# A Fourier layer and two expert layers on one core: raw weights on GpSimd's queue, the tenth chunk of x inside the loop, decode steps and low parts of the first expert block on other engines

## The chip, the core and the metric

One core of a Trainium2 chip runs the whole program. Its engines each work through a list of instructions in order: TensorE (PE; PEld is its weight load), VectorE (DVE), ScalarE (ACT), GpSimd (POOL) and SyncE (SP), which here only issues transfers. ScalarE and GpSimd issue transfers too. The metric is the time of one execution in microseconds of the device, the median of several runs.

## The reference

```python
def _attn_ref(x, w_r, w_i, b_r, b_i):
    X = np.fft.rfft(x, axis=1)
    Yr = Xr @ w_r - Xi @ w_i + b_r
    Yi = Xr @ w_i + Xi @ w_r + b_i
    # soft threshold of both by 0.01
    return np.fft.irfft(Y, n=x.shape[1], axis=1)

def _moe_ref(x, w_in, w_out):
    h = x @ w_in
    return (h - np.tanh(h)) @ w_out

def _moe2_ref(x, w_in, w_out):
    h = x @ w_in
    return (h * np.clip(h + 3.0, 0.0, 6.0) / 6.0) @ w_out
```

The three are applied one after the other. x is 2 x 3008 x 256 in float32, the expert weights are 256 x 2048 and 2048 x 256 in float64.

## The kernel before

**The Fourier layer** runs in four stages: A (47 points, `dft_a`, one chunk of x at a time, 16 chunks, the result stored to DRAM as s1), B (64 points, `dft_b`, on rows read back from s1 into the tiles bi), the linear layer with its threshold (`linear`, `shrink`), C (`dft_c`, stored as s2) and D (`dft_d`). The first eight chunks (batch 0) come before the loop; chunks 8 to 15 (batch 1) share three tiles x1 (called xb in the rows), so chunk i+3 can be loaded only when chunk i is stored. A loop of 24 rounds (t) then runs `linear(t)`, `dft_c(t-2)`, `dft_b(t+2)` and, in the first rounds, one more `dft_a` (from chunk `A0` on, with both halves copied by ScalarE and stored on ScalarE's queue). A chunk before `A0` is stored by a line of its own. Constants of stages B and C come in pieces; those of C on GpSimd's queue, each behind a one-element copy (`gate`) that waits for a tile of the round.

**Every product in the expert layers** is three passes of float32r: high x high, high x low, low x high (lines 112 to 114), so each operand is split: ScalarE writes the high part (line 108, or 446), VectorE or GpSimd subtracts it from the source for the low part (line 109, or 451).

**The expert layers** run in 16 blocks of tokens (k) and 8 groups of hidden units (g), as 2 x 2 block products with seven multiplications (p1 to p7) in place of eight. A group makes al, be and ga in PSUM; ScalarE copies s1, s5 and su out of them (lines 633, 637, 645), VectorE adds them up to c11, c12 and c22 (635, 647, 655), and each of these goes through the nonlinearity (`nl`: ScalarE's activation, line 468, then VectorE's subtraction, line 469) and a split (`nl_split`). The four output products of group g run on TensorE within group g+1. The fourth sum, c21, stays in al and is treated at the start of the next group (`tail_nl`). A bank's next product can start only when ScalarE's copy of the last one is done. GpSimd prepares operands of the next block (`prep_early`: subtractions of line 428, low parts of line 451).

**The weights** arrive as raw 64-bit numbers (512 KB pieces, three buffers) and are decoded to float32 and split by a generator, `w_steps`, one step a call: ScalarE rescales the high words (line 165) and converts the low ones (168), VectorE masks (170), merges (183), adds (199), forms the sums for the block products (203 to 207); ScalarE writes the high part (180), VectorE the low part (191). Where `fine` holds, the steps are smaller. Steps are called at places of the loop's rounds until `NDEC` pieces are done, and then at the places a to e of a group (`super_hook`). A raw piece is asked for when the merge of an earlier one is on its way (`due`, `w_flush`).

## Time and profile before

| | |
|---|---|
| median of 3 runs | 1187.01 us (1186.61 to 1188.89) |
| the profiled execution | 1187.16 us |
| its span, first to last instruction | 1185.4 us |
| TensorE busy | 1174.0 us |
| VectorE, ScalarE, GpSimd busy | 927.4, 864.8, 170.5 us |
| TensorE's granted clock, all stages | 1.00 of full speed (2.4 GHz) |
| spectral loop and what leads to it | up to 163.9 us |
| first expert block, groups 1 to 7 | 163.9 to 220.5 us |

Busy time of TensorE overlaps from one matmul to the next, so a full share doesn't tell how much it waits. The stretches in which a matmul starts later than the step from one to the next are read from the timeline: start, duration, engine, line, what is written and read, and in square brackets how long the engine was idle before it and what ended that.

### The profile page before, as it was taken

Reading aid. Unit: us, or ns where it says so; the run is one execution under the profiler, and the core shown is the slowest. Engines: PE = TensorE matmul, PEld = TensorE weight load, DVE = VectorE, ACT = ScalarE, POOL = GpSimd, SP = SyncE. Lnnn points to the kernel's source line nnn. Section 1 sums busy time; section 2 is a strip of 40 time slices with the busy share of each in tenths; the row PEclk is TensorE's granted clock in tenths of the full one; section 3 lists DMA queues with packets and bytes.
Section 4 is the critical chain, followed back from the end, with each engine's and each line's share of the span. In section 5 each row is a group of like instructions: output and inputs, shape, how many; then the busy total and the mean of one; then the engine's idle time right before and its main releaser. Section 6 shows DMA issues by size and latency. Waiting matters only on the chain.

```text
span 1185.4 us, 20708 instructions
## 1 busy us (share of the span) xinstructions
PE 1174.0 (99%) x7750; PEld 1158.3 (98%) x7750; DVE 927.4 (78%) x1785; ACT 864.8 (73%) x1808; POOL 170.5 (14%) x176
## 2 busy tenths in 40 slices
PE   8999999999999999999999999999999999999998
PEld 6999999999999999999999999999999999999998
DVE  2589888888888888888877788777777777777776
ACT  2566777787778777777777778777777777777775
POOL 0000010202030111102021412121203030302100
PEclk9999999999999999999999999999999999999999
DMA  8986532012122213122106521000000000010000
GB/s 298 330 310 210 166 93 63 27 63 70 69 76 76 94 58 112 62 72 71 54 1 222 175 95 37 15 28 28 28 28 28 28 26 29 2 54 2 19 9 28
DMA packets 43948, 96.51 MB, mean 81 GB/s; under 512 B 4327, under 2 KB 27879, under 8 KB 43751
## 3 DMA queue, kind: packets, MB, share of 16 engines
q1 hardware_dynamic: 39113, 76.58, 19.5%
q0 software_dynamic: 2864, 13.24, 3.4%
q10 hardware_dynamic: 1870, 5.36, 1.3%
q8 instruction: 61, 1.00, 0.3%
q14 instruction: 40, 0.33, 0.1%
HBM read 58.72 MB, written 36.44 MB: 80 GB/s over the span
## 4 chain that ended last, share of the span: by engine, by line
PE 92%; DVE 3%; DMA 2%; ACT 2%; issue 1%; SPq 0%; ACTq 0%; DVEq 0%
PE acc L112 16%; PE acc L114 16%; PE acc L113 16%; PE al L112 7%; PE al L113 7%; PE al L114 7%; PE be L112 4%; PE be L113 4%; PE be L114 4%; PE ga L112 2%; PE ga L114 2%; PE ga L113 2%; PE ga L414 2%; PE acc L371 1%; DMA s<-xa 1%
## 5 line engine op out<-in xcount | busy, mean ns | idle before, releaser
L109 DVE TENSOR_TENSOR gl<-g,gh 128x376 fp32r<-128x376 f32 (+2 forms) x509 | 291.9, 573 | 154.7 <-ACT gh L108 131.6
L108 ACT ACTIVATE gh<-g 128x376 fp32r<-128x376 f32 (+2 forms) x509 | 262.8, 516 | 153.1 <-DVE g L469 81.1
L113 PE MATMUL acc<-wo,gh 128*128 128x256 f32 x752 | 211.9, 282 | 0.0
L112 PE MATMUL acc<-wo,gh 128*128 128x256 f32 x752 | 211.6, 281 | 0.0
L114 PE MATMUL acc<-wo,gl 128*128 128x256 f32 x752 | 211.3, 281 | 0.0
L112 PE MATMUL acc<-gh,wo 128*128 128x376 f32 x512 | 173.6, 339 | 0.0
L114 PE MATMUL acc<-gh,wo 128*128 128x376 f32 x512 | 171.2, 334 | 0.0
L113 PE MATMUL acc<-gl,wo 128*128 128x376 f32 x512 | 171.0, 334 | 0.0
L114 PEld LDWEIGHTS acc<-wo,gl 128*128 128x128 f32 x752 | 142.8, 190 | 0.0
L113 PEld LDWEIGHTS acc<-wo,gh 128*128 128x128 f32 x752 | 141.9, 189 | 0.0
L112 PEld LDWEIGHTS acc<-wo,gh 128*128 128x128 f32 x752 | 141.7, 188 | 0.0
L471 ACT ACTIVATE e<-c,three 128x384 f32<-128x384 f32 (+1 forms) x192 | 116.6, 607 | 12.7 <-DVE c L647 12.5
L472 DVE SCALAR_TENSOR_TENSOR g<-e,c 128x384 f32<-128x384 f32 (+1 forms) x192 | 105.6, 550 | 15.5 <-ACT e L471 10.5
L469 DVE TENSOR_TENSOR g<-c,e 128x376 f32<-128x376 f32 x189 | 113.8, 602 | 5.0 <-ACT e L468 2.4
L428 POOL TENSOR_TENSOR bmt<-bmt 128x376 f32<-128x376 f32 (+2 forms) x60 | 72.0, 1205 | 289.3 <-ACT bmt L419 289.1
L468 ACT ACTIVATE e<-c 128x376 f32<-128x376 f32 x189 | 97.4, 516 | 11.6 <-DVE c L647 11.2
L112 PEld LDWEIGHTS acc<-gh,wo 128*128 128x128 f32 x512 | 96.3, 188 | 0.0
L113 PEld LDWEIGHTS acc<-gl,wo 128*128 128x128 f32 x512 | 96.3, 188 | 0.0
L114 PEld LDWEIGHTS acc<-gh,wo 128*128 128x128 f32 x512 | 96.2, 188 | 0.0
L637 ACT ACTIVATE s<-be 128x376 f32<-128x376 f32 (+2 forms) x127 | 61.7, 486 | 43.3 <-PE be L114 42.9
L647 DVE TENSOR_TENSOR c<-be,su 128x376 f32<-128x376 f32 (+2 forms) x127 | 69.5, 548 | 19.7 <-ACT su L645 14.9
L645 ACT ACTIVATE su<-al 128x376 f32<-128x376 f32 (+2 forms) x127 | 60.6, 477 | 12.2 <-PE al L114 12.1
(219 smaller groups left out, 2792.0 us busy)
## 6 DMA issues: line engine op xcount, KB each, us to landing
raw<-in_moe_w_in_dram SPq DMA_DIRECT2D x16, 512.0 KB
raw<-in_moe_w_out_dram SPq DMA_DIRECT2D x16, 512.0 KB
w2id<-wout SPq DMA_DIRECT2D x8, 896.0 KB
wi<-w2id POOLq DMA_DIRECT2D x8, 896.0 KB, 4.8
y1d<-y SPq DMA_DIRECT2D x32, 188.0 KB
s<-co SPq DMA_DIRECT2D x23, 256.0 KB
bi<-s SPq DMA_DIRECT2D x11, 512.0 KB
bmt<-y1d SPq DMA_DIRECT2D x7, 768.0 KB
```

Of the source, the lines that this page charges most:

```text
L108: act.activation(out=hi, in_=src, func=ACTF.Copy)
L109: (lo_eng or dve).tensor_tensor(out=lo, in0=src, in1=hi.bitcast(F32), op=ALU.subtract)
L112: pe.matmul(out=out_ap, lhsT=lh, rhs=rh, start=start, stop=False, **kw)
L113: pe.matmul(out=out_ap, lhsT=lh, rhs=rl, start=False, stop=False, **kw)
L114: pe.matmul(out=out_ap, lhsT=ll, rhs=rh, start=False, stop=stop, **kw)
L428: eng.tensor_tensor(out=blkv(k, out), in0=blkv(k, a), in1=blkv(k, b), op=ALU.subtract)
L468: act.activation(out=e, in_=src, func=ACTF.Tanh)
L469: dve.tensor_tensor(out=g, in0=src, in1=e, op=ALU.subtract)
L471: act.activation(out=e, in_=src, func=ACTF.Relu, bias=three)
L472: dve.scalar_tensor_tensor(out=g, in0=e, scalar=6.0, in1=src, op0=ALU.min, op1=ALU.mult)
L637: act.activation(out=s5, in_=be, func=ACTF.Copy)
L647: dve.tensor_tensor(out=c12, in0=be, in1=su, op=ALU.add)
```

## The change

Four things are changed. (1) `A0` is 9: the tenth chunk's transform (chunk 9) moves from before the loop into round 0, its load from ScalarE's queue to SP's, behind the loads of the stored rows bi0 and bi1; the load of chunk 12 moves behind round 0. (2) Until the expert layers begin, raw weights are asked for on GpSimd's queue instead of SP's. (3) In block 0 the decode steps are counted as owed, one at each of a, b and d of a group and two at c, and a step that begins with ScalarE runs only at b or c, one at each; the generator says by what it yields whether its next step is one. `fine` holds from the 14th piece on instead of the 18th, so the rescaling and the conversion of a piece are steps apart. (4) In block 0 the low parts of g11 and g12 are made by GpSimd instead of VectorE.

```diff
@@ -128,13 +128,13 @@
 
-    A0 = 10
+    A0 = 9
     NDEC = 13
...
     w_raw = {}
-    ptr = {"load": 0, "dec": 0, "due": 0}
+    ptr = {"load": 0, "dec": 0, "due": 0, "owed": 0, "scalar": None}
 
@@ -143,7 +143,7 @@
             raw = wst.tile([128, 512], I64, tag="raw", bufs=3, name="raw")
-            sp.dma_start(out=raw, in_=w_src[nm][c].rearrange("p a f -> p (a f)"))
+            (sp if mo else pool).dma_start(out=raw, in_=w_src[nm][c].rearrange("p a f -> p (a f)"))
             w_raw[nm, c] = raw
@@ -154,7 +154,7 @@
         for k, (nm, c) in enumerate(w_order + [(None, 0)]):
-            fine = k > 16
+            fine = k > 12
             if nm:
@@ -164,12 +164,12 @@
                 if fine:
-                    yield
+                    yield True
                 act.activation(out=rnd, in_=lw, func=ACTF.Copy, scale=2.0 ** -29)
-                yield
+                yield not fine
                 dve.tensor_scalar(out=hw, in0=hw, scalar1=0x80000000, scalar2=None, op0=ALU.bitwise_and)
                 if fine:
-                    yield
+                    yield True
             if prev:
@@ -197,7 +197,7 @@
             dve.tensor_tensor(out=ta, in0=ta, in1=rnd, op=ALU.add)
-            yield
+            yield nm[1] == "o"
             src = taf
@@ -206,14 +206,14 @@
                 src = ws[:, 1:8, :].rearrange("p a f -> p (a f)")
-                yield
+                yield True
             n = src.shape[1]
...
     def w_step():
-        next(w_gen, None)
+        ptr["scalar"] = next(w_gen, None)
 
@@ -645,7 +645,7 @@
         dve.tensor_tensor(out=c12, in0=be, in1=su, op=ALU.add)
-        nl_split(k, g, 0, 0, g11)
+        nl_split(k, g, 0, 0, g11, None if k else pool)
         hook("b")
@@ -655,7 +655,7 @@
             g12 = nl(k, c12)
-        nl_split(k, g, 0, 1, g12)
+        nl_split(k, g, 0, 1, g12, None if k else pool)
         g22 = nl(k, c22)
@@ -705,13 +705,13 @@
                 f(a)
-        load_x(9, q=act)
         load_bm(1, act)
...
         load_bi(1)
+        load_x(9)
         dft_a(8)
@@ -725,7 +725,6 @@
         wpool["r"] = ctx.enter_context(tc.tile_pool(name="wr", bufs=1, side="right", reuse_waits="tile"))
-        ab = dft_a(9, False)
         dft_b(0)
@@ -734,11 +733,8 @@
         evict_b_neg(1)
-        dft_a_out(9, ab)
-        store_a(9)
         load_x(11)
         w_load()
-        load_x(12)
         ab = None
@@ -748,8 +744,7 @@
                 dft_b(t + 2)
-            if t:
-                ab = dft_a(a_next, False) if a_next < 16 else None
+            ab = dft_a(a_next, False) if a_next < 16 else None
             if t > 1:
@@ -780,8 +775,7 @@
                 load_cm(t // 2 + 1, s_t[t][0:1, 0, 0:1])
-            if t > 0:
-                load_x(12 + t)
+            load_x(12 + t)
             if t < 2:
@@ -879,9 +873,16 @@
                     prep_early(n, g, pos)
-            if 1 <= g < 6 and k < NS:
-                if k or pos in "abcd" and ptr["dec"] < 16:
-                    w_step()
+            if k == 0 and pos != "e":
+                ptr["owed"] += 2 if pos == "c" else 1
+                free = pos in "bc"
+                for _ in range(min(2, ptr["owed"])):
+                    if ptr["dec"] < 16 and (free or not ptr["scalar"]):
+                        free = free and not ptr["scalar"]
+                        w_step()
+                        ptr["owed"] -= 1
+            if 1 <= g < 6 and 0 < k < NS:
+                w_step()
             if pos == "e" and k in (NS - 1, NS):
```

TensorE ahead of the loop, before (xb1 is chunk 9, xb0 chunk 8, warm a filler):

```order
L688 MATMUL acc_209<-warm_120 128x256 x5
L275 MATMUL al_220<-xb0_100,amt_99 96x256 x2
L275 MATMUL be_223<-xb0_100,amt_99 96x256 x2
L688 MATMUL ga_240<-warm_120 128x256 x2
L275 MATMUL acc_247<-xb1_101,amt_99 96x256 x2
L275 MATMUL acc_250<-xb1_101,amt_99 96x256 x2
L319 MATMUL al_253<-bmt_82,bi0_87 128x128 x4
L319 MATMUL ga_264<-bmt_82,bi0_87 128x128 x4
```

and now:

```order
L688 MATMUL acc_208<-warm_120 128x256 x5
L275 MATMUL al_220<-xb0_100,amt_99 96x256 x2
L275 MATMUL be_223<-xb0_100,amt_99 96x256 x2
L688 MATMUL ga_240<-warm_120 128x256 x2
L319 MATMUL al_247<-bmt_82,bi0_87 128x128 x4
L319 MATMUL ga_258<-bmt_82,bi0_87 128x128 x4
```

The two B stages on bi0 follow the filler directly; chunk 9's four matmuls stand behind the third B stage, in round 0.

ScalarE in the fourth group of block 0 (c11, c12, c22 the sums, gh a high part, ws a decode buffer), before:

```order
L468 ACTIVATE e_1995<-c11_1989 128x376
L165 ACTIVATE ws_1999<-raw_1471 128x512
L168 ACTIVATE ws_1999<-raw_1471 128x512
L645 ACTIVATE su_2014<-al_1971 128x376
L108 ACTIVATE gh_2018<-g_1996 128x376
L180 ACTIVATE wi7_2023<-ws_1826 128x896
L468 ACTIVATE e_2036<-c12_2016 128x376
L108 ACTIVATE gh_2018<-g_2037 128x376
```

and now:

```order
L468 ACTIVATE e_1995<-c11_1989 128x376
L645 ACTIVATE su_2011<-al_1971 128x376
L108 ACTIVATE gh_2015<-g_1996 128x376
L165 ACTIVATE ws_2019<-raw_1471 128x512
L468 ACTIVATE e_2032<-c12_2013 128x376
L108 ACTIVATE gh_2015<-g_2033 128x376
L468 ACTIVATE e_2038<-c22_2030 128x376
L168 ACTIVATE ws_2019<-raw_1471 128x512
```

The rescaling stands behind the first split instead of ahead of su, the conversion behind the second, and the high part of a weight goes to the next group.

GpSimd over block 0 and the preparation of block 1 (bmt are operands, odd block 1's split ones), before:

```order
L109 TENSOR_TENSOR gl_1759<-bi1_88,gh_1758 128x376
L428 TENSOR_TENSOR bmt_82<-bmt_82 128x376 x2
L451 TENSOR_TENSOR odd_2286<-bmt_82,odd_2286 128x376 x3
L428 TENSOR_TENSOR bmt_82<-bmt_82 128x376
L451 TENSOR_TENSOR odd_2286<-bmt_82,odd_2286 128x376
```

and now, from the fifth group on:

```order
L109 TENSOR_TENSOR gl_2203<-g_2183,gh_2202 128x376
L109 TENSOR_TENSOR gl_2203<-g_2220,gh_2202 128x376
L428 TENSOR_TENSOR bmt_82<-bmt_82 128x376 x2
L451 TENSOR_TENSOR odd_2280<-bmt_82,odd_2280 128x376
L109 TENSOR_TENSOR gl_2300<-g_2277,gh_2299 128x376
L109 TENSOR_TENSOR gl_2300<-g_2320,gh_2299 128x376
L451 TENSOR_TENSOR odd_2280<-bmt_82,odd_2280 128x376 x2
L428 TENSOR_TENSOR bmt_82<-bmt_82 128x376
L109 TENSOR_TENSOR gl_2402<-g_2379,gh_2401 128x376
L451 TENSOR_TENSOR odd_2280<-bmt_82,odd_2280 128x376
L428 TENSOR_TENSOR bmt_82<-bmt_82 128x376
L109 TENSOR_TENSOR gl_2402<-g_2420,gh_2401 128x376
```

Two low parts a group now stand in GpSimd's list, and the two subtractions behind those of the fifth group.

## Rows read from the trace of the kernel before

**Rows 1.** The head of the page.

```profile
span 1185.4 us, 20708 instructions
```

**Rows 2.** Timeline of the start: start us, duration us, engine, line, what.

```profile
24.20 1.40 SPq L308 DMA_DIRECT2D bi<-s  x3
...
27.10 1.94 PE L275 MATMUL acc<-xb,amt 128*96 128x256 f32 x8 [1.65 <-DMA xb<-in_x_dram]
...
29.23 0.18 POOL L676 COPY gate<-bi 1x1 f32<-1x1 f32 x1 [28.78 <-DMA bi<-s]
...
29.27 1.13 PE L319 MATMUL al<-bmt,bi 128*128 128x128 f32 x8 [0.22 <-issue]
```

**Rows 3.** Timeline of TensorE in the loop: stage C of four rounds.

```profile
50.51 0.81 PE L371 MATMUL acc<-ly,cmt 128*128 128x256 f32 x3
...
56.85 0.81 PE L371 MATMUL acc<-ly,cmt 128*128 128x256 f32 x3
...
100.18 1.03 PE L371 MATMUL acc<-ly,cmt 128*128 128x256 f32 x4
...
104.81 1.03 PE L371 MATMUL acc<-ly,cmt 128*128 128x256 f32 x4
```

**Rows 4.** Timeline: chunks 11 and 12 asked for, a store, chunk 11 used.

```profile
32.67 0.32 SPq L259 DMA_DIRECT2D xb<-in_x_dram  x1
...
34.92 0.33 ACTq L296 DMA_DIRECT2D s<-xb  x1
...
44.93 0.31 SPq L259 DMA_DIRECT2D xb<-in_x_dram  x1
...
45.92 1.03 PE L275 MATMUL be<-xb,amt 128*96 128x256 f32 x4
```

**Rows 5.** Stretches: us, busy by engine (count), TensorE's clock, DMA share, GB/s.

```profile
24.00:26.00 2.00, 1.45 (x7) 0.92 (x5) 1.37 (x3) 1.39 (x3) 0.00 (x0) 1.00 0.78 283
...
40.00:45.00 5.00, 5.00 (x35) 4.63 (x34) 1.96 (x4) 2.02 (x5) 0.00 (x0) 1.00 0.93 314
```

**Rows 6.** DMA issues: destination and source, queue, count, size of one.

```profile
raw<-in_moe_w_in_dram SPq DMA_DIRECT2D x16, 512.0 KB
...
xb<-in_x_dram ACTq DMA_DIRECT2D x1, 512.0 KB
```

**Rows 7.** Timeline of ScalarE and of TensorE near 72 us.

```profile
70.05 0.67 ACT L165 ACTIVATE ws<-raw 128x512 f32<-128x512 f32 x1 [1.58 <-DMA raw<-in_moe_w_out_dram]
...
72.67 1.10 PE L275 MATMUL al<-xb,amt 128*96 128x256 f32 x4 [0.34 <-ACT xb L288]
```

**Rows 8.** Timeline of TensorE, first expert block: its start, a wait, its end.

```profile
163.91 0.34 PE L112 MATMUL al<-even,wi 128*128 128x376 f32 x1
164.08 0.33 PE L113 MATMUL al<-even,wi 128*128 128x376 f32 x1
...
186.03 0.44 PE L112 MATMUL al<-t3h,wi 128*128 128x376 f32 x1 [0.67 <-ACT su L645]
...
220.46 0.33 PE L112 MATMUL al<-odd,wi 128*128 128x376 f32 x1
```

**Rows 9.** Timeline of ScalarE in the first expert block.

```profile
180.06 0.52 ACT L108 ACTIVATE gh<-g 128x376 fp32r<-128x376 f32 x1 [1.46 <-DVE g L469]
...
181.72 0.52 ACT L108 ACTIVATE gh<-g 128x376 fp32r<-128x376 f32 x1 [0.73 <-DVE g L469]
...
184.39 0.66 ACT L165 ACTIVATE ws<-raw 128x512 f32<-128x512 f32 x1
...
185.50 0.47 ACT L645 ACTIVATE su<-al 128x376 f32<-128x376 f32 x1
```

**Rows 10.** Timeline: low parts on GpSimd and on VectorE.

```profile
164.93 0.99 POOL L109 TENSOR_TENSOR gl<-bi,gh 128x376 fp32r<-128x376 f32 x1 [76.45 <-ACT gh L108]
...
167.38 1.31 DVE L109 TENSOR_TENSOR gl<-g,gh 128x376 fp32r<-128x376 f32 x1
...
180.62 0.55 DVE L109 TENSOR_TENSOR gl<-g,gh 128x376 fp32r<-128x376 f32 x1 [0.58 <-ACT gh L108]
```

## The prediction

> **What bounds the kernel now.** I began with the busy shares and the chain that ended last, and both give TensorE nearly the whole span, which is 1185.4 us [rows 1]. A busy TensorE is not yet one at its best, so I then read its own timeline, for starts that stand further apart than the usual step: 0.17 us from one 376-column matmul to the next (163.91, 164.08) [rows 8]. Few do. At the start TensorE waits 1.65 us for the tenth chunk of x, which lands at 27.10, and 0.22 us more until the first stored rows (bi) are there [rows 2]. In the spectral loop it waits once, at 72.67, some 0.5 us beyond the step. In the first expert block it waits several times: the seven groups from 163.91 to 220.46 take 56.55 us [rows 8]; a group has 45 such matmuls, 7 x 45 x 0.172 = 54.2, so 2.3 us are waiting. Behind that, nothing that the change touches waits. All that it can win is therefore 2.3 + 0.5 us, and what it makes of the start; the rest of the question is what it costs.
>
> **The start.** Before, the tenth chunk's transform stands on TensorE ahead of the first B stage, which begins at 29.27; the stored rows that it needs were asked for at 24.20, and GpSimd's gate copy, which waits for the same rows, runs at 29.23 [rows 2]. So rows and transform are ready together. The change takes the transform away from there, and its 512 KB [rows 6] away from in front of the rows. The B stage then waits for the rows alone. At the rate of that moment, 283 GB/s [rows 5], 0.524 MB are 1.85 us, so the rows land between 29.23 - 1.85 = 27.4 (all of it was in their way) and 29.2 (none). I take 27.7, near the early end, since the chunk was asked for ahead of the rows and landed ahead of them. The transform isn't gone: it becomes part of the loop's first round. A round with a transform takes 56.85 - 50.51 = 6.34 us, one without 104.81 - 100.18 = 4.63 [rows 3], so it costs 1.71 there, and the loop has no slack to hide it. Sum: 27.7 + 1.71 - 29.27 = **+0.14 us** (-0.16 to +1.65). What was a free filling of a wait is now paid, and the wait's end comes earlier by about as much.
>
> **The twelfth chunk.** The raw weights leave SP's queue for GpSimd's. On SP the first of them stood behind the twelfth chunk of x (asked for at 32.67) and behind a thirteenth that waits until 44.93 for a store that ScalarE asked for at 34.92, ten microseconds for one store: the transfers are that crowded [rows 4]. On GpSimd's queue three of them, 512 KB each [rows 6], hang on gates alone: the first is asked for with the first stored rows, the other two some 8 us after it, by my estimate 5 to 10 us sooner than on SP's. They take turns with SP's transfers while those still carry two large stores and the twelfth chunk. TensorE used that chunk at 45.92 without a wait [rows 4]. No row shows when it landed. By the bytes asked for since 24.20, at the rates of the windows, the engines on the average reach its end at about 43, and the slowest later, perhaps just ahead of 45.92. One raw chunk ahead of it costs 0.524 MB at 314 GB/s [rows 5] = 1.7 us, two cost 3.3. With the start's +0.14 TensorE wants it at 46.06. So the wait is between 0 (it had 3 us of slack) and 3.2 (none, two chunks ahead). I take **+0.8 us**: nearly one chunk ahead of it, about half of that in slack. It would not be won back, since the loop is bound by TensorE from there on.
>
> **The wait at 72.67.** TensorE waits for ScalarE's copy of the transform; ScalarE had itself waited 1.58 us, until 70.05, for a raw chunk [rows 7], which SP had asked for late since it was stuck behind a chunk of x. GpSimd's queue has only gates and constants in it, and no load of x. I count **-0.5 us** (0 to -0.5).
>
> **First expert block, what goes.** ScalarE's two rescaling steps stood between the activation of c11 and the copy su: 184.39 to 185.50 [rows 9], and TensorE, which reuses that bank, started at 186.03 instead of 185.2, 0.8 us late [rows 8]. They are now taken apart and put behind the two splits of the group, one at each, where su is already done. VectorE loses two low parts a group, 0.55 us each [rows 10]. And GpSimd's two subtractions for the next block, which before ran far ahead, at the block's start, and stretched VectorE's low part at 167.38 to 1.31 us [rows 10], now stand behind the low parts, at the fifth group. All of this together could end all 2.3 us.
>
> **First expert block, what comes.** A low part takes 0.99 us on GpSimd [rows 10]. That VectorE's ran 1.31 us instead of 0.55 while GpSimd worked shows that they exclude each other: 0.76 us lost in one meeting. So the subtraction that follows on VectorE (it reads c and e, both in SBUF) must wait for GpSimd's low part. ScalarE's second split of a group and the next one are 181.72 - 180.06 = 1.66 us apart now [rows 9]; with a low part of 0.99 in between and VectorE's step released only then, I make it 2.04, +0.38 a group. The chain through a group (activations, subtractions, splits, back to the copy s) was about 6.8 us, and is 7.2 then, under the 45 x 0.172 = 7.75 that TensorE takes. It holds in a group without decode work on VectorE. Where a decode burst of some 2 us follows (third and fifth group) it doesn't: I find waits of 0.4 and 0.24 us there when I lay the rows' durations one behind the other. In groups six and seven GpSimd's queue now has the two subtractions, four low parts of the next block's operands, two more subtractions and the four low parts moved to it: twelve pieces of about a microsecond in two groups, 15.5 us. They meet VectorE at nearly every step; the same laying out gives TensorE waits of 0.5 and 0.75 us in the seventh group, which has none now. With 0.18 that stays at the start, 0.18 + 0.4 + 0.24 + 1.25 = 2.1 us of waiting against 2.3: **-0.2 us**. Bounds: -1.9 (only the 0.4 is left) to +1.7 (the last groups cost twice that, and the next block starts on a late operand).
>
> The Trainium skill says of this in "SBUF — State Buffer", "Who interferes with whom", that a VectorE instruction with two SBUF inputs and a GpSimd instruction that reads SBUF shut each other out for a whole instruction, whichever comes second. The trace agrees: 1.31 us against 0.55. By that rule alone, with every moved low part blocking VectorE and none fitting beside its PSUM reads, the block would be the rival below.
>
> Nothing else moves the time: the banks of the transforms change places with one another, the decode steps of later blocks stand where they stood, and a gate copy of GpSimd in front of a raw load waits for a step of the same round.
>
> **Sum.** The profiled execution took 1187.16 us, 0.15 over the median of 1187.01. 1187.16 + 0.14 + 0.8 - 0.5 - 0.2 = 1187.40; against the median, 1187.01 + 0.24 = 1187.25, which I round to **1187.3 us**.
>
> **Rivals.**
> The crowded start (slower): raw weights on GpSimd's queue take turns with SP's transfers, the twelfth chunk lands after 48.5 and TensorE waits 2.5 to 3.2 us. For it: no engine is idle of transfers there (314 GB/s at 40 to 45 us, [rows 5]). Against it: the slack isn't known. It decides from a wait of about 2.5 us; with 3.2, 1187.01 + 0.14 + 3.2 - 0.5 - 0.2 = 1189.7. Chance 0.13. The Trainium skill states in "DMA: Bandwidth & Descriptors", "Issuing engines are not separate DMA queues", that transfers of all queues run on the same 16 engines and interleave; by that rule another queue brings no bandwidth, and this rival is its price. The ten microseconds of ScalarE's store beside SP's full queue agree [rows 4].
> The lock in the last groups (slower): the twelve pieces on GpSimd cost TensorE 3 us there and at the next block's start rather than 1.25, so the block is at +1.7 to +2: 1187.01 + 0.14 + 0.8 - 0.5 + 2 = 1189.5. For it: 0.76 us in a single meeting [rows 10]. Against it: VectorE steps that read PSUM lie beside most pieces. Chance 0.13.
> The block cleared and the chunk in time (faster): 1187.01 + 0.14 - 0.5 - 2.3 = 1184.4. For it: the largest wait there is named and removed. Against it: VectorE's chain gets longer. Chance 0.13.
> The rows don't come earlier (the reorder doesn't do what it says): +1.65 at the start, then no wait for the twelfth chunk: 1187.01 + 1.65 - 0.5 - 0.2 = 1188.0. For it: something other than the tenth chunk may hold the rows. Chance 0.10.
> My forecast, a wash within 0.2%: 0.51.
>
> **How the numbers follow.** A difference of 0.2% (2.4 us) is about what a measurement here can tell from none. Faster is the third rival, 0.13; slower the first two, 0.26; same is the forecast and the fourth, 0.61. The range goes from just above the third rival's time to a little past the first's, 1184.6 to 1190.2: it leaves out about a tenth at each end.
>
> **What would show it.** Right: the first B stage starts near 27.7; TensorE's transform of the twelfth chunk starts 0 to 2 us late with a wait on a DMA; no wait near 72 us; in the first block waits at the first matmul of p7 in groups three and five, and in group seven, while VectorE's low parts and subtractions of 1 us and more stand beside GpSimd's. Wrong: a first block with no waits at all (faster by over 2 us), a twelfth chunk more than 2.5 us late, or a B stage that still starts at 29.

## The result, and the profile after

The changed kernel takes **1195.18 us** (median of 7 runs, 1191.43 to 1198.47) against 1188.60 of the kernel before, measured beside it: a ratio of 1.0058 (95% interval 1.0045 to 1.0071), slower by 0.6%. The forecast was 1187.3, in a range up to 1190.2. The profiled execution of after took 1193.28 us, 6.1 more than that of before, and its span is 6.1 us longer as well. The head of its page, which answers [rows 1]:

```profile
span 1191.5 us, 20738 instructions
...
PE 1174.5 (99%) x7750; PEld 1159.1 (97%) x7750; DVE 925.7 (78%) x1770; ACT 866.3 (73%) x1809; POOL 195.2 (16%) x207
```

TensorE's busy time is what it was; the 6 us are waiting, and a stretch at half clock. Where they lie, the timeline of after shows (start, duration, engine, line, what; in brackets the idle time before it and what ended it). It answers [rows 2] and [rows 4]:

```profile
26.73 0.18 POOL L676 COPY gate<-bi 1x1 f32<-1x1 f32 x1 [26.28 <-DMA bi<-s]
...
26.77 1.13 PE L319 MATMUL al<-bmt,bi 128*128 128x128 f32 x8 [1.48 <-issue]
...
27.57 0.57 POOL L146 DMA_DIRECT2D raw<-in_moe_w_in_dram  x1
...
33.41 0.32 SPq L259 DMA_DIRECT2D xb<-in_x_dram  x1
...
44.26 1.05 PE L319 MATMUL al<-bmt,bi 128*128 128x128 f32 x8
...
49.31 1.99 PE L275 MATMUL ga<-xb,amt 128*96 128x256 f32 x4 [3.99 <-DMA xb<-in_x_dram]
...
51.09 1.51 PE L275 MATMUL al<-xb,amt 128*96 128x256 f32 x4
...
57.06 1.03 PE L275 MATMUL al<-xb,amt 128*96 128x256 f32 x4
```

The stored rows land earlier and the first B stage starts at 26.77 instead of 29.27: 2.5 us won. Then the twelfth chunk of x, asked for at 33.41, isn't there. Undisturbed, its transform starts 0.89 us behind the B stage ahead of it (45.03 to 45.92 in the kernel before); here that stage starts at 44.26 and the transform at 49.31, 4.2 us late. And what follows is slow: the next round's transform starts 7.75 us behind this one (49.31 to 57.06), where a round takes 6.34 [rows 3]. That is 1.4 us more, and the stretches of after show why (columns: the stretch, busy time by engine, then TensorE's granted clock, the share of the transfer engines, GB/s); they answer [rows 5]:

```profile
24.00:26.00 2.00, 1.29 (x6) 0.76 (x4) 1.54 (x3) 1.23 (x3) 0.00 (x0) 1.00 0.69 232
...
28.00:30.00 2.00, 1.50 (x13) 1.30 (x11) 0.69 (x1) 1.24 (x4) 0.13 (x1) 1.00 0.77 176
40.00:45.00 5.00, 5.00 (x39) 4.76 (x38) 1.93 (x4) 1.92 (x4) 0.00 (x0) 1.00 1.01 371
48.00:50.00 2.00, 0.69 (x2) 0.58 (x3) 0.00 (x0) 0.00 (x0) 0.00 (x0) 0.66 1.03 318
```

From 48 to 50 us the granted clock is 0.66 on the average: behind the long wait TensorE works at 1.2 GHz for a while. Before, the same stretch moved more:

```profile
28.00:30.00 2.00, 1.78 (x11) 1.26 (x10) 0.00 (x0) 0.00 (x0) 0.77 (x2) 1.00 0.96 274
```

At 28 to 30 us it is now 176 GB/s at a share of 0.77 instead of 274 at 0.96, and from 40 us on it is more than before (371 against 314), at a share of 1.01. The totals alone don't show which transfer is in the way; the experiments ask that.

The first expert block, answering [rows 8], on TensorE:

```profile
167.59 0.34 PE L112 MATMUL al<-even,wi 128*128 128x376 f32 x1
...
188.77 0.44 PE L112 MATMUL al<-t3h,wi 128*128 128x376 f32 x1 [0.73 <-ACT su L645]
...
213.69 0.44 PE L112 MATMUL al<-t3h,wi 128*128 128x376 f32 x1 [0.94 <-ACT su L645]
...
226.03 0.34 PE L112 MATMUL al<-odd,wi 128*128 128x376 f32 x1
...
231.59 0.43 PE L112 MATMUL al<-t3h,wi 128*128 128x376 f32 x1 [0.73 <-ACT su L645]
```

It begins 3.68 us later than before, takes 58.44 us instead of 56.55, and the next block starts with a wait at p7 (231.59) that was not there; from its first matmul to TensorE's last it takes 960.71 us instead of 960.01. 3.68 + 1.89 + 0.70 = 6.3, against 6.1 of the span.

### The profile page after: what moved, and what is told of

The parts are those of the page before. It is cut to its first block, busy times and chain, and to the rows that moved or that the text cites. A ratio compares the mean times of both kernels' runs of the same rounds, so it can differ in the third digit from the quotient of the medians.

```text
span 1191.5 us, 20738 instructions
## 1 busy us (share of the span) xinstructions
PE 1174.5 (99%) x7750; PEld 1159.1 (97%) x7750; DVE 925.7 (78%) x1770; ACT 866.3 (73%) x1809; POOL 195.2 (16%) x207
## 4 chain that ended last, share of the span: by engine, by line
PE 90%; DVE 3%; ACT 3%; DMA 2%; issue 1%; POOL 1%; SPq 0%; DVEq 0%; ACTq 0%; POOLq 0%
PE acc L112 16%; PE acc L114 15%; PE acc L113 15%; PE al L112 7%; PE al L113 7%; PE al L114 7%; PE be L112 3%; PE be L113 3%; PE be L114 3%; PE ga L414 2%; PE ga L112 2%; PE ga L114 2%; PE ga L113 2%; PE acc L371 2%; DVE g L469 1%; DMA xb<-in_x_dram 1%
## 5 line engine op out<-in xcount | busy, mean ns | idle before, releaser
L109 DVE TENSOR_TENSOR gl<-g,gh 128x376 fp32r<-128x376 f32 (+2 forms) x495 | 283.3, 572 | 150.0 <-ACT gh L108 127.0
L469 DVE TENSOR_TENSOR g<-c,e 128x376 f32<-128x376 f32 x189 | 117.8, 623 | 13.0 <-ACT e L468 10.6
L471 ACT ACTIVATE e<-c,three 128x384 f32<-128x384 f32 (+1 forms) x192 | 116.5, 607 | 12.4 <-DVE c L647 12.2
```

The lines of the kernel that those rows point to most:

```text
L109: (lo_eng or dve).tensor_tensor(out=lo, in0=src, in1=hi.bitcast(F32), op=ALU.subtract)
L469: dve.tensor_tensor(out=g, in0=src, in1=e, op=ALU.subtract)
L471: act.activation(out=e, in_=src, func=ACTF.Relu, bias=three)
```

## The experiments

First each part alone on the kernel before, then the parts undone one by one on the changed kernel, then what of each part does it. Ratios are to the kernel before, measured beside it each time; "late" is by how much TensorE's transform of the twelfth chunk starts beyond its step of 0.89 us in the profiled execution; "block" is from the second group's first matmul (163.91 in [rows 8]) to the first of the next block, "rest" from there to TensorE's last matmul.

| kernel | median us | ratio (95%) | late, us | block, us | rest, us |
|---|---|---|---|---|---|
| before | | | 0 | 56.55 | 960.01 |
| after: all four parts | 1195.18 | 1.0058 (1.0045 to 1.0071) | 4.2 | 58.44 | 960.71 |
| raw weights on GpSimd's queue alone | 1186.74 | 0.9999 (0.9990 to 1.0008) | 0.6 | 56.54 | 959.97 |
| tenth chunk moved alone | 1187.83 | 1.0007 (0.9999 to 1.0016) | 1.2 | 56.53 | 960.02 |
| decode steps' places alone | 1186.66 | 0.9985 (0.9975 to 0.9996) | 0 | 56.07 | 960.23 |
| low parts on GpSimd alone | 1189.48 | 1.0012 (1.0000 to 1.0024) | 0 | 58.02 | 960.78 |
| places and raw weights | 1186.75 | 0.9991 (0.9980 to 1.0002) | 2.4 | 56.06 | 960.27 |
| after, raw weights back on SP | 1191.50 | 1.0039 (1.0024 to 1.0053) | 0 | 58.50 | 960.79 |
| after, low parts back on VectorE | 1191.76 | 1.0031 (1.0019 to 1.0044) | 4.6 | 56.09 | 960.30 |
| after, both back | 1187.95 | 1.0010 (0.9999 to 1.0021) | 1.9 | 56.36 | 960.25 |

The four parts alone add up to +0.03%, together they cost 0.58%: most of the loss is in how they meet.

### Theory A and its rival: raw weights or the tenth chunk

Theory A: the raw pieces on GpSimd's queue crowd the twelfth chunk. Rival: the tenth chunk's load does, which now stands behind the rows. Raw weights back on SP's queue in the changed kernel:

```diff
-            (sp if mo else pool).dma_start(out=raw, ...)
+            sp.dma_start(out=raw, ...)
```

> The changed kernel with the raw weights back on SP's queue; all else as changed. Theory A (the raw pieces on GpSimd's queue are asked for early and crowd the twelfth chunk of x): TensorE's 4.2 us wait for that chunk near 49 us shrinks to under 0.5 us, the granted clock stays at 2.4 GHz through the loop, the wait near 72 us (0.5 us) comes back, and the time falls by 5 to 7 us from the changed kernel's 1195.2, to 1188.2 to 1190.2. Rival (the tenth chunk's load, now on SP's queue and behind the stored rows, is what delays the twelfth): the wait stays above 3 us and the time above 1193.

The raw weights alone (the opposite edit on the kernel before):

> The kernel before with the raw weights on GpSimd's queue until the expert layers begin; nothing else. Theory A: TensorE waits 2.5 to 5 us for the twelfth chunk near 46 us, with or without a stretch at half the granted clock behind it (1.5 to 4 us), and the time is 1191 to 1196 against 1188.6 before. Rival (it needs the tenth chunk behind the rows as well): a wait under 0.5 us there, and 1188.1, since the 0.5 us wait near 72 us goes.

The tenth chunk alone (`A0 = 9`, `load_x(9)` behind the rows, `load_x(12)` behind round 0):

> The kernel before with the tenth chunk's load behind the stored rows and its transform in round 0; nothing else. Theory A: the first B stage starts at 26.8 instead of 29.3, a transform costs 1.7 us in the loop, the twelfth chunk comes in time: 0.8 us faster, 1187.5 to 1188.2. Rival: TensorE waits over 2.5 us for the twelfth chunk, and the time is 1190 or more.

TensorE's timeline, with the raw weights alone moved (the B stage, then the transform):

```profile
44.85 1.05 PE L319 MATMUL al<-bmt,bi 128*128 128x128 f32 x8
...
46.31 1.07 PE L275 MATMUL be<-xb,amt 128*96 128x256 f32 x4 [0.40 <-DMA xb<-in_x_dram]
```

with the tenth chunk alone moved:

```profile
44.57 1.05 PE L319 MATMUL al<-bmt,bi 128*128 128x128 f32 x8
...
46.70 1.07 PE L275 MATMUL ga<-xb,amt 128*96 128x256 f32 x4 [1.08 <-DMA xb<-in_x_dram]
```

and in the changed kernel with the raw weights back:

```profile
46.44 1.05 PE L319 MATMUL al<-bmt,bi 128*128 128x128 f32 x8
...
47.33 1.03 PE L275 MATMUL ga<-xb,amt 128*96 128x256 f32 x4
```

The long wait goes when the raw weights go back, as theory A said; but the time falls by 2.3 us (1.0058 to 1.0039) and not by 5 to 7. In that profiled execution TensorE started the first B stage at 28.95, 2.2 us later than in after's, so part of the chunk's time was hidden there, and the low parts cost more than I had allowed for. And neither single part makes the 2.5 us that its crowding side expected (nor is the moved chunk alone the 0.8 us faster that theory A gave it): each costs little alone, and each alone makes a wait.

How much slack the chunk had can be read. Beside the rows, the trace keeps the landing events of a load (its semaphore rises sixteen times), and in all eleven executions in which TensorE waited for this chunk it starts 0.13 to 0.14 us behind the last of them. Before, that event is at 45.07 and TensorE starts at 45.92, so the slack was 0.7 us. With the raw weights alone moved the chunk lands at 46.17, with the tenth chunk alone at 46.57, with all parts at 49.17: 1.1, 1.5 and 4.1 us later. Either move uses up the slack, and in these executions both together take more than the sum. Each is a single execution: in two more with the old order the chunk lands at 42.48 and 43.72, so 1.1 and 1.5 are no more than one execution can differ from another by itself, and 4.1 is.

The two moves don't delay it in the same way. The twelfth chunk takes the tile of the ninth, so SP asks for it only when the ninth's store is through. With the tenth chunk alone moved that comes late, at 36.79 instead of 32.67 [rows 4], though the chunk is then under way for only 9.8 us, against 12.4 before:

```profile
25.96 0.36 SPq L296 DMA_DIRECT2D s<-xb  x1
...
36.79 0.32 SPq L259 DMA_DIRECT2D xb<-in_x_dram  x1
```

With the raw weights alone moved it is asked for at 33.15 and under way for 13.0 us; with all parts, at 33.41 and 15.8 us.

### Which raw piece

Three pieces go to GpSimd's queue early: the first at 27.57, two more near 36. I held the second and third back until the twelfth chunk has landed:

```diff
+            if t == 0:
+                pool.tensor_copy(out=gate[0:1, 0:1], in_=x1[0][32:33, 0, 0:1])
             if t < 2:
                 w_load()
```

> The changed kernel in which GpSimd asks for the second and third raw piece only when the twelfth chunk of x has landed; both stay on GpSimd's queue, and the first piece is asked for as early as in the changed kernel. Theory A (these two, 1 MB asked for at 35.6 and 36.2 us, take turns with the twelfth chunk): the wait for the chunk falls from 4.2 to between 0.5 and 2 us, the clock stays at 2.4 GHz, and the time falls by 3.5 to 5.5 us. Rival (the first piece does it, or the stores): the wait stays above 3 us and the time within 1 us of the changed kernel's.

The ratio was 1.0036 (1.0020 to 1.0053), 2.6 us better, between the two theories. TensorE's timeline still has the wait, 3.5 us beyond the step:

```profile
44.75 1.05 PE L319 MATMUL al<-bmt,bi 128*128 128x128 f32 x8
...
49.11 1.99 PE L275 MATMUL ga<-xb,amt 128*96 128x256 f32 x4 [3.31 <-DMA xb<-in_x_dram]
```

and the stretches of that run show that TensorE waits while the transfer engines are mostly idle (their share is 0.38, then 0.14; the columns are those of above):

```profile
46.00:48.00 2.00, 0.00 (x0) 0.00 (x0) 0.69 (x1) 1.13 (x3) 0.00 (x0) 1.00 0.38 152
48.00:50.00 2.00, 0.89 (x2) 0.68 (x3) 0.00 (x0) 0.00 (x0) 0.58 (x2) 0.57 0.14 50
```

So theory A fell in the form that I had given it: not the two pieces that are under way together with the chunk, but what stands ahead. Next the first piece alone back on SP's queue, behind the chunk:

```diff
-            (sp if mo else pool).dma_start(out=raw, ...)
+            (sp if mo or ptr["load"] == 1 else pool).dma_start(out=raw, ...)
```

> The changed kernel with the first raw piece alone back on SP's queue, behind the twelfth chunk of x; the second and third stay on GpSimd's, asked for near 36 us. Holding back the second and third took only 0.7 us off TensorE's 4.2 us wait for that chunk. Theory D (the first piece, asked for at 27.6, is the one that goes ahead of the chunk: 0.524 MB, 1.7 us at 314 GB/s): the wait falls to between 1.3 and 2.8 us, and the time by 1.5 to 4 us, most of it where the stretch at half clock goes as well. Rival (each piece delays it by itself, or what was held back came too late to tell): the wait stays at 3.5 us or more and the time within 1 us of the changed kernel's.

Ratio 1.0027 (1.0016 to 1.0038): 3.7 us of the changed kernel's loss is gone. TensorE's timeline:

```profile
43.62 1.05 PE L319 MATMUL al<-bmt,bi 128*128 128x128 f32 x8
...
45.13 1.08 PE L275 MATMUL ga<-xb,amt 128*96 128x256 f32 x4 [0.46 <-DMA xb<-in_x_dram]
...
54.31 1.07 PE L275 MATMUL al<-xb,amt 128*96 128x256 f32 x4 [2.61 <-DVE ws L204]
```

The wait for the twelfth chunk is 0.6 us beyond the step, even shorter than expected; 2.8 us of it has moved to the thirteenth (54.31; the releaser named is VectorE's, but that tile is a chunk of x asked for at 47.39, whose last landing event is at 54.17). So the waiting itself is only 0.8 us shorter, 3.4 instead of 4.2; but the clock stays at 2.4 GHz through both waits, and that saves another 1.4 in the profiled execution. Is it GpSimd's queue, or the bytes? The first piece as early, but on SP's queue (its old call, behind `load_x(11)`, is taken out):

```diff
-            (sp if mo else pool).dma_start(out=raw, ...)
+            (sp if mo or ptr["load"] == 1 else pool).dma_start(out=raw, ...)
...
         load_bm(2)
+        w_load()
...
         load_x(11)
-        w_load()
```

> The changed kernel with the first raw piece on SP's queue, but as early as it is asked for on GpSimd's: behind the third stage's constants, ahead of two large stores and of the twelfth chunk. If it is the bytes ahead of the chunk that count (theory D): TensorE waits 2.5 to 5 us for the chunk, as in the changed kernel, and the time is within 1.5 us of the changed kernel's, 0.4 to 0.7% over before. If it is GpSimd's queue that goes ahead: the wait is under 2 us and the time as with the piece behind the chunk, 0.2 to 0.3% over before.

Ratio 1.0050 (1.0036 to 1.0065). The timeline: the piece asked for, the twelfth chunk asked for, and the wait, 4.6 us beyond the step:

```profile
28.89 0.78 SPq L146 DMA_DIRECT2D raw<-in_moe_w_in_dram  x1
...
37.28 0.32 SPq L259 DMA_DIRECT2D xb<-in_x_dram  x1
...
44.94 1.05 PE L319 MATMUL al<-bmt,bi 128*128 128x128 f32 x8
...
50.38 1.90 PE L275 MATMUL ga<-xb,amt 128*96 128x256 f32 x4 [4.39 <-DMA xb<-in_x_dram]
```

An early first piece makes the wait on either queue. The Trainium skill states in "DMA: Bandwidth & Descriptors", "Issuing engines are not separate DMA queues", that all issuing engines' transfers run on the same 16 engines. The trace agrees, 4.6 us on one queue and 4.2 on the other. That it is the bytes alone isn't shown: on SP's queue the piece also puts off the chunk's request, from 33.41 to 37.28, and the chunk is then under way for 13.0 us instead of 15.8.

The other half, the tenth chunk's load back at its old place (its transform stays in round 0):

```diff
+        load_x(9, q=act)
         load_bm(1, act)
...
-        load_x(9)
```

> The changed kernel with the tenth chunk's load back on ScalarE's queue at its old place, ahead of the stored rows; its transform stays in round 0 and the raw pieces on GpSimd's queue. Theory D (by its late load the chunk leaves 24 to 30 us at 176 to 255 GB/s and goes ahead of the twelfth instead): the first B stage starts at 27.5 to 29, the wait for the twelfth chunk falls from 4.2 to between 1 and 3 us, and the time by 1 to 3 us. Rival (the place of that load doesn't matter to the twelfth chunk): the wait stays at 3.5 us or more, less what the B stage starts later.

Ratio 1.0035 (1.0022 to 1.0048), 2.7 us of the loss gone, as theory D has it. By the wait it is inconclusive: in the profiled execution the first B stage only started at 32.59, behind a wait of 3.34 us and at half clock, so TensorE came late to the twelfth chunk and found it there. The request does tell something: from the ninth chunk's store to SP's request for the twelfth chunk it takes 6.8 us here (29.68 to 36.51), as in the five kernels with the old order and the request at its old place (6.8 to 7.4), and 7.9 to 10.8 in the nine with the tenth chunk's load moved.

### Theory B and its rival: low parts or decode steps

Theory B: GpSimd's low parts and VectorE shut each other out. Rival: the decode steps' places load VectorE in bursts, whoever makes the low parts. The low parts back on VectorE in the changed kernel:

```diff
-        nl_split(k, g, 0, 0, g11, None if k else pool)
+        nl_split(k, g, 0, 0, g11)
...
-        nl_split(k, g, 0, 1, g12, None if k else pool)
+        nl_split(k, g, 0, 1, g12)
```

> The changed kernel with the two low parts of block 0 back on VectorE; all else as changed. Theory B (GpSimd's low parts and VectorE shut each other out, and that is what the first expert block loses): the first seven groups of block 0 fall from 58.4 to between 55.0 and 56.5 us, the wait at block 1's first p7 goes, and the time falls by 2 to 4 us, to 1191 to 1193. Rival (the new places of the decode steps load VectorE in bursts, whoever makes the low parts): the groups stay above 57.5 us and the time within 1 us of 1195.2.

The opposite edit on the kernel before:

> The kernel before with the two low parts of block 0 on GpSimd alone; the decode steps stay at their old places. Theory B: the seven groups of block 0 take 58 us or more instead of 56.55, VectorE's subtractions of line 469 there take 0.8 to 1.2 us beside GpSimd's low parts, block 1's first group waits 0.5 us or more at p7, and the time is 2 to 3.5 us over before. Rival (only both together cost): the groups take under 57 us and the time is within 0.7 us of before.

The decode steps' places alone on the kernel before (`fine`, the yields, `owed`):

> The kernel before with the decode steps of block 0 at their new places alone; the low parts stay on VectorE, nothing else moves. Theory B (the places help, the low parts on GpSimd cost): TensorE's wait of 0.67 us at the third group's p7 goes, the seven groups of block 0 take 55.5 to 56.5 us instead of 56.55, and the time is within 1 us of before. Rival (the new places cost by themselves): the seven groups take 57 us or more, and the time is 0.5 to 2 us over before.

The block's begin and end on TensorE, with the low parts alone on GpSimd:

```profile
164.90 0.33 PE L112 MATMUL al<-even,wi 128*128 128x376 f32 x1
...
222.92 0.34 PE L112 MATMUL al<-odd,wi 128*128 128x376 f32 x1
...
228.50 0.43 PE L112 MATMUL al<-t3h,wi 128*128 128x376 f32 x1 [0.74 <-ACT su L645]
```

and with the places alone:

```profile
163.44 0.33 PE L112 MATMUL al<-even,wi 128*128 128x376 f32 x1
...
184.81 0.44 PE L112 MATMUL al<-t3h,wi 128*128 128x376 f32 x1 [0.62 <-ACT su L645]
...
219.50 0.34 PE L112 MATMUL al<-odd,wi 128*128 128x376 f32 x1
```

Theory B holds: the low parts cost and the places don't. The low parts alone make the block 1.47 us longer and the rest 0.77; the places alone make the block 0.48 shorter and the rest 0.22 longer. The block's time is the same to 0.1 us in all kernels with the same two parts but one (56.36), whatever happened ahead of it, so these are the most certain numbers here. By time the low parts cost 1.4 us alone (0 to 2.9), less than I expected, and 3.2 us in the changed kernel (1.0058 against 1.0031). But the wait at the third group's p7 didn't go with the places, as theory B also had it: 0.62 us at 184.81, as 0.67 before [rows 8].

How the low parts do it, the groups of instructions on VectorE show, over 163.9 to 226 us. In the kernel before (line, operation, count, busy us, mean ns, then the idle time before them):

```profile
L469 DVE TENSOR_TENSOR g<-c,e 128x376 f32<-128x376 f32 x22 | 13.0, 590 | 0.3
```

and in the changed kernel:

```profile
L469 DVE TENSOR_TENSOR g<-c,e 128x376 f32<-128x376 f32 x21 | 15.8, 751 | 8.3 <-ACT e L468 8.3
L170 DVE TENSOR_SCALAR raw<-raw 128x512 uint32<-128x512 uint32 x3 | 2.0, 680 | 0.0
```

The subtraction behind the activation takes 0.75 us on the average instead of 0.59. Its timeline, with GpSimd's:

```profile
191.68 1.00 POOL L109 TENSOR_TENSOR gl<-g,gh 128x376 fp32r<-128x376 f32 x1 [1.05 <-ACT gh L108]
...
192.09 0.99 DVE L469 TENSOR_TENSOR g<-c,e 128x376 f32<-128x376 f32 x1 [1.05 <-ACT e L468]
...
208.56 2.43 POOL L428 TENSOR_TENSOR bmt<-bmt 128x376 f32<-128x376 f32 x2
...
208.93 1.21 DVE L170 TENSOR_SCALAR raw<-raw 128x512 uint32<-128x512 uint32 x1
...
210.06 1.34 DVE L109 TENSOR_TENSOR gl<-g,gh 128x376 fp32r<-128x376 f32 x1
```

192.09 falls into GpSimd's low part and ends 0.4 us behind it: 0.99 us instead of 0.55. That is the meeting for which the prediction took 0.38 us a group; ScalarE's second split of that group and its next one are now 2.10 us apart, and were 1.66 [rows 9], so it is 0.44:

```profile
191.08 0.52 ACT L108 ACTIVATE gh<-g 128x376 fp32r<-128x376 f32 x1 [0.62 <-DVE g L469]
...
193.18 0.52 ACT L108 ACTIVATE gh<-g 128x376 fp32r<-128x376 f32 x1 [0.61 <-PE ga L114]
```

### Both undone, and the harmless two together

> The changed kernel with both suspects undone: raw weights on SP's queue, low parts of block 0 on VectorE; the tenth chunk's move and the decode steps' places stay. The two theories together: no wait over 1.5 us for the twelfth chunk, the seven groups of block 0 at 56.1 us, and the time within 1.2 us of before. Rival (something else in the change costs as well): 2 us or more over before.

By the ratio 1.2 us over before, within what was expected and not clear of no difference (0.9999 to 1.0021), though the wait for the twelfth chunk was 1.9 us, a little over: the two suspects hold all of the loss but about a tenth of a percent.

> The kernel before with the two parts that did no harm alone: the decode steps' new places in block 0 and the raw weights on GpSimd's queue. Expected, if they add: no wait for the twelfth chunk over 1 us, the seven groups of block 0 at 56.1 us, the wait near 72 us under 0.4 us: 0.5 to 2 us under before. Rival (the raw pieces cost once the start varies): the time is not under before.

0.9991 (0.9980 to 1.0002): not shown to be faster. In its profiled execution the twelfth chunk is 2.4 us late, against 0.6 with the raw weights alone, so the rival has a point: with the raw pieces early, the wait differs by 1.8 us between two executions whose loops are the same. The places alone are the one version here that beats both kernels, by 0.15%; only 0.3 us of these 1.8 is in the block and behind it, and where the rest is from stays open (the kernel before itself had medians from 1186.92 to 1188.60 over these measurements, and 1188.28 beside this one).

### Theory C: the clock behind the wait

Nine filler matmuls ahead of the twelfth chunk's transform, in the changed kernel:

```diff
+            if t == 2:
+                keep_warm(9, "acc")
             ab = dft_a(a_next, False) if a_next < 16 else None
```

> The changed kernel with nine filler matmuls (3.9 us of TensorE's time, results thrown away) just ahead of the twelfth chunk's transform, where TensorE waits 4.2 us for the chunk. Theory C (the wait makes the chip take TensorE's clock down to 1.2 GHz for a stretch behind it, 1.5 us in the profiled run of the changed kernel, up to 5 us in its slower runs): the granted clock stays at 2.4 GHz, the four matmuls of line 275 behind the wait take their usual 0.22 us apart, and the time falls by 1.5 to 4 us from the changed kernel's, 4 to 7 us over before to 2 to 4. Rival (the clock falls for another reason, the load of the 16 transfer engines or the step of the program): half clock stays, and the time stays or rises.

Ratio 1.0030 (1.0018 to 1.0042), 3.3 us better, as the theory has it. The mean granted clocks fit it too: 0.998 to 1.000 in the nine executions beside the profiled one, five of them at 1.000, against 0.995 to 1.000 in the seven of the changed kernel, one at 1.000. But in the profiled execution the second B stage had waited for rows and run at half clock at 29 us, and the chunk was in time (it landed at 45.63, ahead of the filler's start at 48.55); that trace doesn't show the filler at work. So I made the wait in the kernel before, by the order of SP's queue alone:

```diff
-        load_x(11)
         w_load()
         load_x(12)
...
                 load_bm(t // 2 + 3)
+                if t == 0:
+                    load_x(11)
```

> The kernel before with the twelfth chunk of x asked for behind the thirteenth and a constant on SP's queue; nothing else. TensorE should wait 3 to 5 us for it near 46 us. Theory C (a wait of that length brings a stretch at half the granted clock behind it): a stretch of 3.4 us or more at 1.2 GHz in the records behind the wait, at least 1.5 us lost in it, and the time 4.5 to 9 us over before. Rival (the clock fell for another reason): full clock behind the wait, and the time over before by the wait alone, 3 to 5 us.

Ratio 1.0046 (1.0034 to 1.0058). The timeline:

```profile
50.86 1.99 PE L275 MATMUL be<-xb,amt 128*96 128x256 f32 x4 [5.35 <-DMA xb<-in_x_dram]
52.65 1.92 PE L275 MATMUL al<-xb,amt 128*96 128x256 f32 x4
...
59.52 1.03 PE L275 MATMUL al<-xb,amt 128*96 128x256 f32 x4
```

The stretch behind that wait, by the granted clock (first number behind the engines):

```profile
50.00:56.00 6.00, 5.14 (x18) 4.07 (x19) 0.00 (x0) 1.60 (x3) 0.00 (x0) 0.53 1.04 325
```

A wait alone, with no raw piece moved, brings the half clock: 8.66 us for the round (50.86 to 59.52) instead of 6.34, 2.3 us lost. With the same filler in that wait:

> The same late chunk, with nine filler matmuls (3.9 us) on TensorE just ahead of its transform, in the wait. Theory C: the clock stays at 2.4 GHz, TensorE loses the filler's time or the wait, whichever is longer, and the kernel is 1.5 us or more faster than the one without the filler. Rival: no faster than without the filler.

Ratio 1.0046 (1.0033 to 1.0059): no faster than without. In its profiled execution the filler (49.30 to 53.2) was not enough, 3.45 us of waiting were left behind it, and half clock followed again. But that execution was the slowest of six (1199.55). In the other five the mean granted clock is 0.998 to 1.000, where all five without the filler have 0.996 or 0.997: the clock did stay higher, and the time was no better (1191.33 to 1194.39 against 1192.51 to 1194.33). So the clock's fall behind a long wait is shown, and its price in one execution can be read (1.4 us in the changed kernel's, 2.3 here). That a filler keeps the clock up in most executions can be read from these means; that it wins the time back is shown for the changed kernel alone, by the time and not by a trace, and why it won nothing here stays open.

## Why the prediction was wrong, by its own steps

**What bounds the kernel**: right. TensorE does, and every wait that came on it went into the time.

**The start**: +0.14 us said, -0.8 measured (26.77 + 1.71 - 29.27). The transform's 1.71 was right. The rows were there 0.9 us sooner than the 27.7 that I took, and 0.6 sooner than the early bound; and 29.27, against which I counted, was late: four of the six other profiled executions with the old order start the first B stage at 28.14 to 28.70 (the other two at 31.4 and later, behind a stretch at half clock), so the gain over most of them is 0.6 to 1.1 us smaller. The price of the move saw only one of its ends: it took the 512 KB away from in front of the rows and didn't put them down in front of the twelfth chunk. The tenth chunk alone makes that one 1.2 us late.

**The twelfth chunk**: the step that failed. It read "I take +0.8 us: nearly one chunk ahead of it, about half of that in slack", with 3.2 us as the outer bound. It cost 4.2 us of waiting and 1.4 us at half clock, 5.6 in the profiled execution, and by the clocks more in others: over the seven executions the mean granted clock lies between 0.995 and 1.000, and the one at 1.000 is the fastest (1191.43). The slack in the sum was not what failed: it took about 0.9 us, without a row and so by luck, and 0.7 was there. The delay was. It was put at nearly one piece's 1.7 us, and the chunk landed 4.1 us later than before (49.17 against 45.07). Three things were missing. The tenth chunk's load, now nearer to the twelfth's, was no term at all, and alone it makes the twelfth 1.5 us later in its execution. The pieces were counted wrongly: I thought of those asked for beside the chunk, but holding these back took 0.7 us off the wait, and putting the first behind the chunk, asked for 6 us ahead of it, took 3.5 off, of which 2.8 came back at the thirteenth. And the clock's fall was no term of mine. Why the two moves together cost so much more than each alone stays open; part of it is one straggler, since fifteen of the sixteen landing events were in by 46.31 and the last came 2.9 us behind them. The rival that I called the crowded start named this mechanism and gave it 0.13 and 1189.7; by its sign ("a twelfth chunk more than 2.5 us late") it is the one that came, at 5.6 instead of 3.2, and not by the raw pieces alone.

**The wait at 72.67**: right. No start near there is beyond its step in after, and it stays (0.53 us) with the raw weights on SP. From the B stage behind the twelfth chunk's round (51.37 before, 56.17 after) to the expert block the loop is 1.1 us shorter, 0.5 of it this wait; where the rest is from I haven't found.

**The first expert block**: -0.2 us said, +1.9 measured, and +0.7 in the block behind it, beyond the upper bound of 1.7. Half of the step held: the chain of a group grows by 0.4 us where VectorE's subtraction meets GpSimd's low part; waits stand at p7 of the third group (188.77, 0.9 us; I had 0.4), of the fifth (0.3; 0.24) and in the seventh (0.5 and 0.6; 0.5 and 0.75). What was missed: 1.1 us at p7 of the sixth group (213.69), behind GpSimd's two subtractions (208.56), beside which VectorE's mask of a raw piece takes 1.21 us instead of 0.43 (208.93) and the low part behind it 1.34; and the 0.9 us of the next block's first p7. That the mask, with one input, could be held up I had not thought of. And "all of this together could end all 2.3 us" of the gains was far too kind: the places alone end 0.5.

**The sum**: -0.8 + 5.6 - 1.1 + 1.9 + 0.7 = 6.3, against 6.1 of the span and 0.24 forecast. 4.8 us of the miss are the twelfth chunk's, 2.8 the expert block's with its successor; the start and the loop came out 1.5 better.

## What to carry to other kernels

A transfer that is moved goes out of one transfer's way and into another's: price it at both ends, and price two such moves together, since each may use up the same slack that the other counts on. A load that lands in time has no wait to be read, but its landing events may be in the trace: read the slack there before pricing it, and price the delay by everything that goes ahead of the load, its own request included. And a wait on TensorE costs more than its length when the granted clock falls behind it.

## What was not expected of the hardware

- The granted clock fell to 1.2 GHz behind waits of 3.31, 3.45, 3.99, 4.39, 4.43 and 5.35 us at this place, and stayed at 2.4 behind 1.73, 2.21 and 2.61 there and at the thirteenth chunk. At the start it fell behind one of 2.50 (the low parts alone), one of 3.34 (the tenth chunk's load back) and two of 1.23 and 1.52 close together (the changed kernel's filler run). At this place it cost 1.4 to 2.9 us a time, by the round behind it. The Trainium skill tells of such a fall behind transfer waits in "TensorE: Matmul & The Clock Gate", "HAM oscillation — how this bites in real kernels"; the trace agrees, 0.66 of full speed at 48 to 50 us.
- VectorE's `tensor_scalar` on a raw piece, with one input, took 1.21 us beside GpSimd's subtraction instead of 0.43. The Trainium skill counts that operation among those that can shut GpSimd out or be shut out in "SBUF — State Buffer", "Who interferes with whom"; the trace agrees, though a single meeting stands for it.
- The last of a transfer can trail far behind the rest of it. In the changed kernel and the three of its versions that waited over 3 us for the twelfth chunk (low parts back, later pieces held back, first piece early on SP's queue), fifteen of the chunk's sixteen landing events are in 1.3 to 2.9 us before the last; in the old order with the chunk asked for late it is 0.1. With the later pieces held back, the transfer engines were busy for 0.38 of their time, then 0.14, from 46 us on, until the chunk had landed at 48.98. Why one part trails stays open.
